# FNet mixing and an ELU layer on one core: batch 0's x by plain loads, batch 1 in the small-matmul form

## The chip, the cores and the metric

The kernel runs on one core of a Trainium2 chip. The metric is the time of one execution in device microseconds (us). Three runs of the kernel before gave 1906.94 us as the median (1906.89 to 1907.48).

## What is computed

```python
# x [8, 3008, 256] float32, w_in [256, 2048] and w_out [2048, 256] float64
X = np.fft.fft(x, axis=1)
X = np.fft.fft(X, axis=2)
t = X.real.reshape(8 * 3008, 256)
h = t @ w_in
g = np.where(h > 0.0, h, np.exp(np.minimum(h, 0.0)) - 1.0)
out = (g @ w_out).astype(np.float32)
```

A Fourier transform over the sequence and over the channels, of which the real part is kept, and then a two-layer network of width 2048 on each of the 24064 rows.

## The kernel before

**Stages.** The network takes the rows in 376 steps. A step multiplies the transformed rows by w_in (results in the PSUM bank H), applies the ELU to them (tiles E, M, G on ScalarE, VectorE and GpSimd) and multiplies G by w_out into the banks pA, pB, pC, pD. The first steps do this with plain products (`w`); later ones with sums of rows and of weights (`WT`), which need fewer products. Every step needs rows that are already transformed, so the transform of a batch must be done ahead of its steps; that of batch 0 stands ahead of everything.

**The transform of one batch.** Sequence positions s, 1504-s, 1504+s and 3008-s, for s from 0 to 752, are laid over each other, and so are channels d and 256-d. Tile `xl0` holds rows s upward, `xl1` rows 3008-s downward, `xl2` rows 1504-s downward, `xl3` rows 1504+s upward; partition p holds six rows, numbers 0 to 3 of groups of four and 4 to 5 of groups of two. Sums and differences of the four tiles and of the two channel halves give four operands of 128 x 768 (in the code `EO`). Each is multiplied by a cosine or sine table (`MC`, 128 x 1887, in an even half of 756 and an odd half of 1131 columns): R for the real and I for the imaginary part, each for even and odd frequencies. Such a product is the class `Dft`: an even half of 3 matmuls and an odd half of 3. Beside these four, `x_even` and `x_odd` transform channel 128 alone (`xe`). Batches 0 and 1 take this form. Batches 2 to 7 take another, the class `Quarter`: the sequence is folded once more, and the operands are multiplied by small tables (`QM`, 94 to 96 rows, 94 or 95 columns), 4 matmuls for a half. It costs more additions on VectorE and GpSimd (`mirror_sum`, `half_sum`, `channel_fold`, and the functions called by `quarter_pairs`, `shift_pairs`, `turn_pairs`).

**How x of batch 0 comes in.** `load_x` reads the forward rows (`xl3`, `xl0`) by two DMAs each, on SyncE's queue (SP): 128 pieces of 4 KB, and of 2 KB. The mirrored rows (`xl2`, `xl1`) are read by four gathers that GpSimd issues (`indirect_dma_start`, with row numbers in the table `ix`). `fold_x` then makes the channel sums e0 to e3 and differences o0 to o3 of each tile, and adds and subtracts these (E0, EO0 and so on), 16 VectorE instructions on 768 elements, two of them cut in two.

**Batch 1.** Its x comes by the same two kinds of load (events `L`, `L0` to `L3`). `mirror_folds` gives GpSimd 30 instructions for its sums: 12 on 255 elements of a partition, 2 small ones, 8 on 384 (the tiles), 8 on 384 (the channel halves). Its four `Dft`s stand at steps 26, 34, 37 and 42.

**Weights.** w_in and w_out are float64 in memory and are converted on chip, in chunks `w0` to `w5`, `u0` to `u5`: load, then about ten instructions on 512 elements of a partition, on VectorE, ScalarE and GpSimd (in the trace the tiles raw, w, pow).

**What sets the order.** Each piece of work has a model time (`at(t, fn)`, in steps of T); sorted by it, the pieces are written out, and every engine runs its instructions in that written order. For the first seven steps the table `FRONT` names the pieces: `e3` is one of the sums above; `x-even`, `x-odd`, `R-even` and so on are the halves of the transforms; `R-sum`, `R-up`, `R-down` combine the halves on VectorE; `w0b` is a part of a chunk; `h`, `P`, `Q`, `g`, `V`, `b`, `x` are parts of a step. PE, the matmul engine, starts with 46 matmuls on zeros (`idle`), which nothing reads.

**Waits of DMAs.** The DMAs of the SP and ScalarE queues take eight semaphores in turn (DMAHW0 to DMAHW7), so a DMA waits, before it is issued, until the one that had its semaphore has landed.

Of the kernel before, what the change touches and what calls it, by code (L numbers as in the profile page):

```python
# [17 lines left out]
SEQ = 3008  # L18
# [21 lines left out]
def _dft_consts():  # L40
# [6 lines left out]
    p = np.arange(128)[:, None]  # L47
# [130 lines left out]
def kernel(  # L178
# [33 lines left out]
    def xrows(b, row, step, n, rows=6):  # L212

        return bass.AP(
            tensor=xt,
            offset=x.offset + (b * SEQ + row) * ND,
            ap=[[step * ND, n], [1, rows * ND]],
        )


# [3 lines left out]
    def row_tables():  # L224

        for c, n, base, step in (
            (0, 128, HALF - 3, -4),
            (1, 128, HALF - 513, -2),  # L230
            (2, 128, HALF - 3, -4),
            (2, 1, HALF - 4, 0),
        ):
            pin(
                nc.gpsimd.iota(
                    ix[0:n, c : c + 1],
                    pattern=[[0, 1]],
                    base=base,
                    channel_multiplier=step,
                )  # L240
            )

    def load_x(b):
# [6 lines left out]
        def back(j, few):  # L250
            cols = slice(0, 2 * ND) if few else slice(2 * ND, 6 * ND)
            c = 1 if few else 0
            pin(
                nc.gpsimd.indirect_dma_start(
                    out=L[j][:, cols],
                    out_offset=None,
                    in_=xflat,
                    in_offset=bass.IndirectOffsetOnAxis(
                        ap=ix[:, c : c + 1].bitcast(U32), axis=0
                    ),  # L260
                    element_offset=(b * SEQ + (HALF if j == 1 else 0)) * ND,
                )
            )
        def ahead(j, row):
            nc.sync.dma_start(out=L[j][:, 0 : 4 * ND], in_=xrows(b, row, 4, 128, 4))
            nc.sync.dma_start(
                out=L[j][:, 4 * ND :], in_=xrows(b, row + 512, 2, 128, 2)
            )

        loads = [lambda n=n: back(2 - n // 2, n % 2) for n in range(4)]  # L270
        return L, loads + [lambda: ahead(3, HALF), lambda: ahead(0, 0)]


# [95 lines left out]
    class Chunk:  # L369
# [7 lines left out]
        def load(self):  # L377
# [6 lines left out]
            if not wide:  # L384
                nc.sync.dma_start(out=dst, in_=self.src)
                return
# [3 lines left out]
            nc.sync.dma_start(  # L390
                out=words.rearrange("p (a b) -> p a b", a=n), in_=self.src.bitcast(I32)
# [192 lines left out]
    row_tables()  # L584
# [115 lines left out]
    def sum_weights(i):  # L700
# [5 lines left out]
        b11, b12 = w2v[:, 2 * i, 0:128], w2v[:, 2 * i, 128:256]  # L706
        b21, b22 = w2v[:, 2 * i + 1, 0:128], w2v[:, 2 * i + 1, 128:256]
        W = [t[:, i] for t in WT]
# [6 lines left out]
    def fold_x(L, engine_of, cuts_of):  # L715

        ops = {}

        def op(key, o, a, b, f):
            tt = lambda o, a, b, f: pin(  # L720
                engine_of(key).tensor_tensor(out=o, in0=a, in1=b, op=f)  # L721
            )
            cuts = cuts_of(key, o.shape[1])
            for i in range(len(cuts) - 1):
                c = slice(cuts[i], cuts[i + 1])
                ops[key, i] = lambda c=c: tt(o[:, c], a[:, c], b[:, c], f)

        E, O = [], []
        for j in range(4):
# [6 lines left out]
            if j in (1, 2):  # L736
                src = src[:, ::-1]
# [968 lines left out]
    for load in loads[:5]:  # L1706
        load()
# [490 lines left out]
```

## Time and profile before

| what | value |
| --- | --- |
| median of three runs | 1906.94 us |
| profiled execution | 1907.16 us |
| its span in the trace | 1905.4 us, so 1.76 us lie outside |
| PE busy | 1898.3 us |
| VectorE (DVE), ScalarE (ACT), GpSimd (POOL) busy | 1232.0, 1391.4, 1353.1 us |
| granted PE clock | 1.00 |

Times are in microseconds from the start of the span, unless a column says ns. A timeline row gives start, duration, engine, source line, operation, output and input tiles, shape, count, and in brackets the idle time before it with what ended it. Where rows of one engine follow each other closely, the distance between two starts is the cost, since an instruction's own duration overlaps the next. A matmul of float32 leaves two records, so "x6" is three matmuls. A window row gives start and end, length, busy time of PE, PEld (the weight loads), DVE, ACT and POOL with their counts, the granted clock, the mean busy share of the 16 DMA engines and GB/s.

### The profile page before, as it was taken

To read this page: it belongs to the slowest core of one execution; us is meant where nothing else is said; L and a number is where in the kernel's file an instruction comes from. 1 tells how busy PE (TensorE), PEld (TensorE's weight loads), DVE (VectorE), ACT (ScalarE), POOL (GpSimd) and SP (SyncE) were. 2 spreads that over 40 slices of the span, in tenths; PEclk is the share of its full clock that TensorE was granted. 3 is DMA by queue.
4 is the path that set the end of the run, shared out by engine and by line. 5 is a ranking of instruction groups with operands and counts; after the bars stand their busy time and mean duration, and the time that the engine had idled before them with its cause. 6 is when DMAs were issued, how large, how long until landed. Compare 5 with 4: busy or idle time off the path is not lost.

```text
span 1905.4 us, 28620 instructions
## 1 busy us (share of the span) xinstructions
PE 1898.3 (100%) x8972; PEld 1656.8 (87%) x8972; DVE 1232.0 (65%) x2174; ACT 1391.4 (73%) x2803; POOL 1353.1 (71%) x1846
## 2 busy tenths in 40 slices
PE   9999999999999999999999999999999999999999
PEld 6888888888888888888888888888888888888887
DVE  8755555667666676667766677666776667655445
ACT  5767667777777777777777777777777777777775
POOL 4888658786687766777667777687766777556664
PEclk9999999999999999999999999999999999999999
DMA  8145211211011110211102111022110210100101
GB/s 340 45 33 43 55 24 45 53 24 36 12 44 41 32 33 12 47 40 30 31 19 50 35 27 31 13 56 44 24 24 16 55 21 15 17 12 15 20 11 24
DMA packets 278901, 73.66 MB, mean 39 GB/s; under 512 B 254382, under 2 KB 268972, under 8 KB 278750
## 3 DMA queue, kind: packets, MB, share of 16 engines
q1 hardware_dynamic: 270110, 61.40, 15.9%
q0 software_dynamic: 6464, 10.18, 1.7%
q8 instruction: 71, 1.16, 0.3%
q14 instruction: 80, 0.66, 0.1%
q10 hardware_dynamic: 2176, 0.26, 0.1%
HBM read 46.92 MB, written 24.80 MB: 38 GB/s over the span
## 4 chain that ended last, share of the span: by engine, by line
PE 96%; DVE 2%; ACT 1%; issue 0%; DMA 0%; POOL 0%; ACTq 0%; POOLq 0%; DVEq 0%
PE H L621 37%; PE pB L621 17%; PE pD L621 17%; PE pC L621 17%; PE pA L621 9%; DMA xl<-in_x_dram,ix 0%; DVE e L721 0%; ACT G L633 0%; DVE o L721 0%; POOL w L630 0%; DVE G L1431 0%; DVE E L1401 0%; ACT M L633 0%; ACT E L633 0%; DVE pow L462 0%
## 5 line engine op out<-in xcount | busy, mean ns | idle before, releaser
L630 POOL TENSOR_TENSOR G<-G 128x256 f32<-128x256 f32 x1437 | 1047.4, 737 | 498.0 <-DVE G L1431 358.5
L1431 DVE SCALAR_TENSOR_TENSOR G<-G,H 128x512 f32<-128x512 f32 x376 | 258.2, 687 | 554.5 <-ACT G L633 554.5
L633 ACT ACTIVATE G<-H 128x512 f32<-128x512 f32 x376 | 224.5, 597 | 259.0 <-DVE G L1415 255.4
L621 PE MATMUL H<-Rr,Wsc 128*128 128x256 f32 x1504 | 388.7, 381 | 1.0 <-ACT Wsc L633 0.5
L621 PE MATMUL H<-Ir,Wsc 128*128 128x256 f32 x1504 | 386.7, 380 | 0.7 <-DVE E L1401 0.7
L633 ACT ACTIVATE H<-Rb,wex 128x256 f32<-128x256 f32 x720 | 341.2, 474 | 40.0 <-DVE G L1431 21.5
L621 PE MATMUL pC<-G,WT 128*128 128x256 f32 x1440 | 369.8, 379 | 0.0
L633 ACT ACTIVATE E<-H 128x512 f32<-128x512 f32 x360 | 214.5, 596 | 182.0 <-PE H L621 181.7
L621 PEld LDWEIGHTS H<-Ir,Wsc 128*128 128x128 f32 x1504 | 285.6, 190 | 40.6 <-DVE E L1401 1.5
L621 PEld LDWEIGHTS H<-Rr,Wsc 128*128 128x128 f32 x1504 | 281.7, 190 | 43.1 <-issue 2.3
L621 PEld LDWEIGHTS pC<-G,WT 128*128 128x128 f32 x1440 | 274.2, 190 | 36.6
L1415 DVE SCALAR_TENSOR_TENSOR G<-E,H 128x512 f32<-128x512 f32 x376 | 255.0, 678 | 8.4 <-PE H L621 4.3
L1431 DVE SCALAR_TENSOR_TENSOR G<-M,G 128x512 f32<-128x512 f32 x376 | 256.7, 683 | 0.7 <-ACT M L633 0.7
L633 ACT ACTIVATE G<-G 128x512 f32<-128x512 f32 x376 | 235.0, 625 | 0.0
L621 PE MATMUL pA<-G,w 128*128 128x256 f32 x784 | 229.6, 380 | 0.1
L621 PE MATMUL pB<-G,w 128*128 128x256 f32 x784 | 229.5, 379 | 0.0
L621 PE MATMUL pD<-G,w 128*128 128x256 f32 x784 | 229.4, 379 | 0.0
L633 ACT ACTIVATE M<-G 128x512 f32<-128x512 f32 x376 | 224.4, 597 | 2.8 <-DVE G L1415 2.8
L633 ACT ACTIVATE M<-M 128x512 f32<-128x512 f32 x376 | 222.7, 592 | 0.1
L621 PE MATMUL pB<-G,WT 128*128 128x256 f32 x720 | 214.7, 380 | 0.0
L621 PE MATMUL pD<-G,WT 128*128 128x256 f32 x720 | 214.4, 379 | 0.0
L621 PEld LDWEIGHTS pA<-G,w 128*128 128x128 f32 x784 | 149.2, 190 | 20.6 <-DVE G L1431 0.5
(175 smaller groups left out, 1794.3 us busy)
## 6 DMA issues: line engine op xcount, KB each, us to landing
out_dram<-ot SPq DMA_DIRECT2D x496, 32.0 KB
xq<-in_x_dram SPq DMA_DIRECT2D x48, 94.0 KB
out_dram<-ot SPq DMA_DIRECT2D x256, 2.0 KB
Rb<-r SPq DMA_DIRECT2D x10, 376.0 KB
raw<-in_moe_w_in_dram SPq DMA_DIRECT2D x7, 512.0 KB
MC<-dft_mats SPq DMA_DIRECT2D x3, 943.5 KB
xq<-in_x_dram SPq DMA_DIRECT2D x12, 192.0 KB
xq<-in_x_dram SPq DMA_DIRECT2D x36, 64.0 KB
```

The lines of the kernel that those rows point to most:

```text
L621: nc.tensor.matmul(out_, lhsT=lhsT, rhs=rhs, start=start, stop=stop, skip_group_check=True)
L630: pin(nc.gpsimd.tensor_tensor(out=o, in0=a, in1=b, op=op))
L633: pin(nc.scalar.activation(out=o, in_=i, func=func, **kw))
L1415: nc.vector.scalar_tensor_tensor(out=two(S.G[:, 0:512])[:, :, ::-1], in0=two(S.E), scalar=2.0, in1=two(S.H), op0=ALU.mult, op1=ALU.subtract,)
L1431: nc.vector.scalar_tensor_tensor(out=o, in0=e, scalar=-1.0, in1=h, op0=ALU.add, op1=ALU.max)
```

## The change

**Batch 0's x.** There is no gather. Even and odd rows are loaded apart, even ones first. A forward tile comes by four SP DMAs for each parity, of 64 partitions. A mirrored tile comes by three DMAs for each parity on ScalarE's queue, of 128 partitions with 1 KB each, twelve in all. Such a source is written as two runs of 64 rows that go downward, so partition p holds what partition (p + 64) mod 128 held, and the tables `MC` are permuted alike. The cosine tables' halves are loaded apart too.

On SyncE's queue the program began so before (DMA out<-in and elements of the out tile; "waits" names a semaphore; `raw` and `w_68` are weight chunks, `CC` the channel table):

```order
L265 DMA xl_150<-in_x_dram 128x1024
L266 DMA xl_150<-in_x_dram 128x512
L390 DMA raw<-in_moe_w_in_dram 128x2x512
L265 DMA xl_147<-in_x_dram 128x1024
L266 DMA xl_147<-in_x_dram 128x512
L1710 DMA CC<-chan_mats 128x384
L554 DMA MC_73<-dft_mats 128x756
L554 DMA MC_73<-dft_mats 128x1131
L390 DMA raw<-in_moe_w_in_dram 128x2x512 [waits DMAHW0_49]
```

The two forward tiles and the first weight chunk come first there. Now SyncE's queue begins so (`xl_130` is tile 3, `xl_127` tile 0):

```order
L230 DMA xl_130<-in_x_dram 64x2x256 x2
L230 DMA xl_130<-in_x_dram 64x256 x2
L1646 DMA MC_73<-dft_mats 128x756
L230 DMA xl_127<-in_x_dram 64x2x256 [waits DMAHW2_49]
L230 DMA xl_127<-in_x_dram 64x2x256 [waits DMAHW4_49]
L230 DMA xl_127<-in_x_dram 64x256 [waits DMAHW7_49]
L230 DMA xl_127<-in_x_dram 64x256 [waits DMAHW1_49]
L1660 DMA CC<-chan_mats 128x384 [waits DMAHW3_49]
L373 DMA raw<-in_moe_w_in_dram 128x2x512 [waits DMAHW5_49]
```

Tile 0's loads now wait for loads issued earlier on either queue. ScalarE's instructions, of which only the first two stood at its start before (`xl_129` is tile 2, `xl_128` tile 1):

```order
L617 ACT_TABLE_LOAD
L617 ACTIVATE warm<-warm 128x1 [waits DVE_49]
L230 DMA xl_129<-in_x_dram 128x1x256 x3
L230 DMA xl_128<-in_x_dram 128x1x256 [waits DMAHW0_49]
L230 DMA xl_128<-in_x_dram 128x1x256 [waits DMAHW1_49]
L230 DMA xl_128<-in_x_dram 128x1x256 [waits DMAHW3_49]
L230 DMA xl_128<-in_x_dram 128x1x256 [waits DMAHW5_49]
L230 DMA xl_128<-in_x_dram 128x1x256 [waits DMAHW6_49]
L230 DMA xl_128<-in_x_dram 128x1x256 [waits DMAHW0_49]
L230 DMA xl_129<-in_x_dram 128x1x256 [waits DMAHW2_49]
L230 DMA xl_129<-in_x_dram 128x1x256 [waits DMAHW4_49]
L230 DMA xl_129<-in_x_dram 128x1x256 [waits DMAHW6_49]
```

The mirrored rows moved from GpSimd's gathers to ScalarE's queue, the first weight chunk behind the even rows, and loads of the two queues now wait for each other through the shared semaphores.

**The order of sums.** For each parity the mirrored rows are added to the forward rows first (a3, a0: 765 elements and 3), then the two tiles are added (Z0) and subtracted (Z1: 768 each), and the channel halves are folded from these (E0, O0, E1, O1: 384 each). VectorE's first rows on x before (`xl_150` is tile 3, `xl_149` tile 2, `xl_147` tile 0; e_ and o_ channel sums and differences, w_157 and pow_178 parts of chunk w0):

```order
L721 TENSOR_TENSOR e_174<-xl_150 128x768
L721 TENSOR_TENSOR o_175<-xl_150 128x768
L408 TENSOR_SCALAR pow_178<-raw 128x512
L420 TENSOR_SCALAR w_157<-raw 128x2x256
L450 SCALAR_TENSOR_TENSOR w_157<-raw,w_157 128x2x256
L462 SCALAR_TENSOR_TENSOR pow_178<-raw,pow_178 128x512
L476 SCALAR_TENSOR_TENSOR w_157<-w_157,pow_178 128x2x256
L721 TENSOR_TENSOR e_168<-xl_147 128x512
L721 TENSOR_TENSOR e_172<-xl_149 128x256
```

There the two sums of tile 3 and the chunk's conversion stand ahead of the first mirrored row (`xl_149`). VectorE's first rows now (numbers of tiles as on the queues above, `eo` an operand, w_144 and pow_211 parts of chunk w0; the rows on 3 elements leave out the last size):

```order
L611 TENSOR_TENSOR xl_130<-xl_130,xl_129 128x3x255
L611 TENSOR_TENSOR xl_130<-xl_130,xl_129 128x3
L611 TENSOR_TENSOR xl_127<-xl_127,xl_128 128x3x255
L611 TENSOR_TENSOR xl_127<-xl_127,xl_128 128x3
L611 TENSOR_TENSOR xl_128<-xl_127,xl_130 128x3x256
L611 TENSOR_TENSOR eo<-xl_128 128x3x128 x2
L405 TENSOR_SCALAR w_144<-raw 128x2x256
L393 TENSOR_SCALAR pow_211<-raw 128x512
L435 SCALAR_TENSOR_TENSOR w_144<-raw,w_144 128x2x256
L611 TENSOR_TENSOR xl_130<-xl_130,xl_129 128x3x255
L611 TENSOR_TENSOR xl_130<-xl_130,xl_129 128x3
```

The first instruction now needs both `xl3` and `xl2`, and the chunk's conversion moved behind the even rows' sums.

**PE's start.** Behind the zeros stood before (numbers of tiles: `w_157` chunk w0, `xe` channel 128, MC_73 and MC_74 the tables of even frequencies):

```order
L621 MATMUL H<-w_157,CC 128x256 x4
L621 MATMUL pC<-MC_73,xe_224 128x189 x2
L621 MATMUL pC<-MC_73,xe_224 128x378
L621 MATMUL pD<-MC_73,xe_224 128x377 x3
L621 MATMUL H<-pick,Wsc 128x1 x2
L621 MATMUL pB<-MC_73,e_170 128x377 x3
L621 MATMUL pA<-MC_73,e_170 128x189 x2
```

The weights' product stood first. Now, behind 30 instead of 46 matmuls on zeros:

```order
L605 MATMUL pC<-MC_73,xe_174 128x189 x2
L605 MATMUL pC<-MC_73,xe_174 128x378
L605 MATMUL pA<-MC_73,eo 128x189 x2
L605 MATMUL pA<-MC_73,eo 128x378
L605 MATMUL M<-MC_74,eo 128x189 x2
L605 MATMUL M<-MC_74,eo 128x378
L605 MATMUL H<-w_144,CC 128x256 x4
L605 MATMUL pD<-MC_73,xe_174 128x377 x3
L605 MATMUL pB<-MC_73,eo 128x377 x3
L605 MATMUL pC<-MC_74,eo 128x377 x3
```

The even halves of x, R and I moved ahead of the weights' product; the odd halves, which need odd rows, stand behind it.

**Batch 1** takes the class `Quarter`: `mirror_folds` and its 30 instructions go, and 16 `mirror_sum`, 8 `half_sum`, 16 `channel_fold` and 20 calls of the pair functions come, at times of the table `FIRST`; the four transforms stand at steps 23, 34, 38 and 44 (`QUARTERS`). Its loads change accordingly. `half_sum` is now one instruction in place of two (for all batches), and `sum_weights` is called four times on two chunks in place of eight times on one.

```diff
-    p = np.arange(128)[:, None]
+    p = (np.arange(128)[:, None] + 64) % 128
...
+            if j in (1, 2):
+                for m in (par, 2 + par):
+                    load(t[:, m], r0 - m - 256, [[256 * ND, 2], [-4 * ND, 64]])
+                m = 4 + par
+                load(t[:, m], r0 - 508 - m - 128, [[128 * ND, 2], [-2 * ND, 64]])
+                return
+            for a in range(2):
+                h = slice(64 * a, 64 * a + 64)
+                load(
+                    t[h, par:4:2], r0 + par + 256 * (1 - a), [[4 * ND, 64], [2 * ND, 2]]
+                )
...
-        for m in (2 * h, 2 * h + 1):
-            vtt(o[:, 3 - m], a[:, m], b[:, m], ALU.subtract if kodd else ALU.add)
+        m = slice(2 * h, 2 * h + 2)
+        tt(o[:, 2 - 2 * h : 4 - 2 * h][:, ::-1], a[:, m], b[:, m], ALU.subtract if kodd else ALU.add)
...
-    for _ in range(46):
+    for _ in range(30):
         mm(idle, zero, zero[:, 0:1].to_broadcast([128, 512]), True)
...
+    FIRST_LOADS = 'x20 x30 M000 x00 C w0 x10 x31 x11 M100 x01 M001 x21 M101 w1 p'
...
+    REST_LOADS = 'w2 u0 u2 M01 u1 w4 w3 M11 u5 w5'
...
-        (-20.84, "e3 o3"),
-        (-19.11, "w0a w0b w0p w0R c3"),
+        (-20.84, "xl1 a3e x1 a0e Z0e E0e c0e O0e"),
+        (-18.994, "m0e w0b x-even R-even w0a w0R I-even w0p"),
+        (-16.994, "x-copy a3o w0s w0M f0 a0o Z0o E0o"),
...
-    for step, ri, kodd in ((26, 0, 0), (34, 1, 0), (37, 0, 1), (42, 1, 1)):
-        at_dft(step, 2, 1, ri, kodd, lambda k=2 * ri + kodd: state["EO"][k])
...
+    QUARTERS = ((23, 1, 0, 0, 29), (34, 0, 0, 0, 38), (38, 0, 1, 43, 48), (44, 1, 1, 45, 53))
...
+    for step, ri, kodd, finish, join in QUARTERS:
+        at_quarter(step, 1, ri, kodd, finish, join)
```

In `FIRST_LOADS` a name such as `x20` is tile 2's even rows, `x21` its odd rows, `M001` the odd half of table (0, 0), `w0` a chunk, `C` the channel table.

More of the change, by code (lines that the diff above doesn't have):

```diff
@@ L210, with load_x @@
     xt = x.tensor
[L212 to L218, printed above, removed]
     xflat = x.rearrange("b s d -> (b s) d")
     ix = cpool.tile([128, 6], I32, tag="ix")
[L224 to L243, printed above, removed]
+    def load_x():
         L = [
@@ L375, in __init__, with load @@
             self.shared, self.pairs = shared, pairs
-        def load(self):
+        def load(self, keep=lambda i: i):
             dst = self.dst()
@@ L1889 @@
         at(t, lambda c=c: spread_last_row(c))
-    for i in range(8):
-        at((12.9 + 0.5 * i) * T + 3.6, lambda i=i: sum_weights(i))
+    for n, t in enumerate((13.208, 16.4467, 17.2731, 15.0726)):
+        at(t * T, lambda i=2 * n: sum_weights(i))
     total = n_tiles * 8
```

353 lines of the change are left out of this document (146 added, 207 removed), and 49 rows, old and new, of the table FRONT.

## The prediction

> **What bounds the kernel now.** I read the busy times first, then PE's waits, then the timelines of PE and VectorE over the first 45 us, then DMA windows. From the page:
>
> ```profile
> span 1905.4 us, 28620 instructions
> PE 1898.3 (100%) x8972; PEld 1656.8 (87%) x8972; DVE 1232.0 (65%) x2174; ACT 1391.4 (73%) x2803; POOL 1353.1 (71%) x1846
> ```
>
> PE is busy in all but 7 us of the span. So PE time taken out shortens the program, PE time added lengthens it, and time on other engines counts only where PE waits. PE's waits, largest first:
>
> ```profile
> PE H L621 <- ACT Wsc L633: 1.1, 2, 0.6
> PE M L621 <- DVE zero L581: 1.1, 1, 1.1
> ```
>
> But busy PE is not all useful PE. The start of its timeline, with one later piece:
>
> ```profile
> 1.14 13.12 PE L621 MATMUL M<-zero 128*128 128x512 bf16 x46 [1.14 <-DVE zero L581]
> 14.10 1.89 PE L621 MATMUL H<-w,CC 128*128 128x256 f32 x8
> 15.84 1.54 PE L621 MATMUL pC<-MC,xe 128*128 128x189 f32 x6
> 17.22 2.06 PE L621 MATMUL pD<-MC,xe 128*128 128x377 f32 x6
> 19.12 0.50 PE L621 MATMUL H<-pick,Wsc 128*128 128x1 f32 x4
> ...
> 36.14 1.89 PE L621 MATMUL pA<-G,w 128*128 128x256 f32 x8
> ```
>
> Until 14.10 PE multiplies zeros; x-even starts at 15.84, x-odd at 17.22, and the first product of a step (pA<-G) at 36.14. From there PE runs steps almost without a gap, so a shift of 36.14 goes through to the end. What sets it is VectorE, as its timeline shows:
>
> ```profile
> 5.19 0.96 DVE L721 TENSOR_TENSOR e<-xl 128x768 f32<-128x768 f32 x1 [1.86 <-DMA xl<-in_x_dram]
> 6.07 0.95 DVE L721 TENSOR_TENSOR o<-xl 128x768 f32<-128x768 f32 x1
> 6.94 0.42 DVE L408 TENSOR_SCALAR pow<-raw 128x512 int32<-128x512 int32 x1
> 7.27 0.42 DVE L420 TENSOR_SCALAR w<-raw 128x512 int32<-128x512 int32 x1
> 7.73 0.69 DVE L450 SCALAR_TENSOR_TENSOR w<-raw,w 128x512 f32<-128x512 uint32 x1
> 8.34 0.68 DVE L462 SCALAR_TENSOR_TENSOR pow<-raw,pow 128x512 int32<-128x512 int32 x1
> ...
> 10.85 0.42 DVE L721 TENSOR_TENSOR e<-xl 128x256 f32<-128x256 f32 x1 [0.30 <-DMA xl<-in_x_dram,ix]
> ...
> 25.03 0.54 DVE L627 TENSOR_TENSOR Rb<-bs,pD 128x375 f32<-128x375 f32 x1
> 25.48 0.54 DVE L627 TENSOR_TENSOR Rr<-bs,pB 128x377 f32<-128x377 f32 x1
> ...
> 27.98 0.87 DVE L1401 SCALAR_TENSOR_TENSOR E<-Rb,wex,H 128x256 f32<-128x256 f32 x2
> ...
> 34.34 0.68 DVE L1431 SCALAR_TENSOR_TENSOR G<-M,G 128x512 f32<-128x512 f32 x1
> ```
>
> VectorE works from 5.19 to the end of the first G, 35.02, with idle times of a few tenths: 0.30 for the first gather. Costs between starts: 0.87 us for 768 elements, 0.33 for TENSOR_SCALAR on 512, 0.61 for SCALAR_TENSOR_TENSOR on 512, 0.45 for 377.
>
> **The new loads.** The change takes the gathers away and puts twelve DMAs of 128 x 1 KB = 131 KB on ScalarE's queue, with a source of two runs that go downward. Before, only line 336's loads (94 rows of 1 KB, two runs of 47 downward) are alike; line 319's go forward. Windows on two times of line 336, one of line 319 (96 rows), and the start:
>
> ```profile
> 297.25:298.00 0.75, 0.75 (x5) 0.65 (x5) 0.75 (x2) 0.72 (x3) 0.64 (x1) 1.00 0.13 48
> 299.00:300.50 1.50, 1.50 (x8) 1.33 (x7) 1.12 (x3) 1.18 (x4) 1.42 (x3) 1.00 0.14 48
> 182.50:183.50 1.00, 1.00 (x6) 0.90 (x5) 0.92 (x3) 0.70 (x3) 0.98 (x2) 1.00 0.94 298
> 12.00:20.00 8.00, 7.78 (x36) 5.16 (x35) 7.93 (x16) 2.50 (x8) 0.00 (x0) 1.00 1.05 415
> ```
>
> Line 336's loads keep 0.13 of 16 engines busy, which is two, at 48 GB/s; line 319's keep 0.94 busy at 298 GB/s. The new loads lie between: their source is like the slow ones, their 128 destination rows like the fast ones. So one costs 131 KB / 48 GB/s = 2.73 us or 131 / 298 = 0.44 us. Whether 94 rows or two runs made line 336 slow, no row says, since there both go together. I take 2.73, because only those rows have the same source. The other value is rival A.
>
> The Trainium skill (DMA: Bandwidth & Descriptors, section "Why a DMA increments its semaphore by 16 and not by 1") says that a DMA takes the largest number of engines up to 16 that divides the slowest dimension, other than 1, of both sides. The source's two runs would make that two, the sum below; were the destination alone to count, it would be 16, rival A. The trace agrees at line 336 (0.13), but no run here shows 128 rows against two runs.
>
> **The front, step by step, at 2.73 us a load.** ScalarE's queue can begin behind its table load:
>
> ```profile
> 0.74 1.28 ACT L633 ACT_TABLE_LOAD   x1 [0.74 <-PEq L2182]
> 2.04 0.20 ACT L633 ACTIVATE warm<-warm 128x1 f32<-128x1 f32 x1
> ```
>
> So bytes flow from about 3.3 (an estimate: 2.24 and a second for issue and landing). Twelve loads on two engines: 32.8 us. These engines also carry their sixteenth of SyncE's part ahead of the last of them, 3.07 MB in all (the forward rows, half tables, CC, w0): 192 KB an engine at 415 / 16 = 25.9 GB/s is 7.4 us. Last odd row of `xl2`: 3.3 + 32.8 + 7.4 = 43.5. SyncE's forward rows are no help: each DMA waits for one issued eight earlier on either queue, so the last forward odd rows are issued behind the last but one of ScalarE's, and land near 45.
>
> Then a0 (0.95), Z0 (0.87) and the copy of channel 128: x-odd starts near 47.3 instead of 17.22. Even rows land earlier (six loads and half the rest, about 22.6), x-even runs near 25 instead of 15.84, and PE, with zeros until 10.6 only, stands idle around it. Behind x-odd come the odd halves of R and I, three times 1.9 us (17.22 to 19.12). R-up needs R's: 47.3 + 3.8 = 51.1, or up to 53 if PE comes slow out of its idle time. That it can be slow, the weight loads of the first zeros show:
>
> ```profile
> 6.66 0.15 PEld L621 LDWEIGHTS <-zero 128*128 128x128 bf16 x1 [0.28 <-issue]
> 7.09 6.67 PEld L621 LDWEIGHTS <-zero 128*128 128x128 bf16 x31 [0.28 <-issue]
> ```
>
> One matmul took 0.43 us until 7.09 and 6.67 / 31 = 0.22 after it. I take 1 us for it, with 0 and 2 as ends.
>
> The Trainium skill (TensorE: Matmul & The Clock Gate, Part 1) says that PE idle for a window of about 3.4 us falls back to half its clock. By it the whole 2 us would be paid here; the trace agrees in the first 14 zeros, and no row of it shows a return to the slow rate.
>
> Behind R-up, to the end of the first G, the new order has on VectorE 9 pieces of 375 to 384 elements at 0.45 (two halves of a sum counted as one), 5 TENSOR_SCALAR at 0.33, 6 SCALAR_TENSOR_TENSOR at 0.61 (of G and of weights), one 768 at 0.87, four E pieces at 0.4: 4.1 + 1.7 + 3.7 + 0.9 + 1.6 = 12.0. So G ends near 52 + 12 = 64, and the first pA starts with it: 64 - 36.1 = +28.
>
> Covers in this stretch. The remaining weights and tables (w1, w2, u0, the table M01) stand behind these loads on SyncE; they start near 45 and move at 415 GB/s: 2.6 MB by their shapes, 6.3 us, so until 52, when VectorE is at R-up. M01 is first used after it, w1 shortly before: cover nearly gone, up to +3. GpSimd loses four gathers; VectorE's 0.30 us wait was for one of them. The removed 16 zeros and the shorter sums (16 x 768 elements become 4 x 768 + 4 x 768 + 8 x 384, 4.3 us less at 0.87 for 768) lie in time when everything waits for rows, and bring nothing here.
>
> **Batch 1.** From PE's timeline: an even and an odd half of `Dft` with what followed each, and a half of `Quarter`:
>
> ```profile
> 173.00 1.44 PE L621 MATMUL H<-MC,eo 128*128 128x189 f32 x6
> 174.28 1.03 PE L621 MATMUL H<-Rr,Wsc 128*128 128x256 f32 x4
> ...
> 184.63 2.07 PE L621 MATMUL H<-MC,eo 128*128 128x377 f32 x6
> 186.54 1.03 PE L621 MATMUL H<-Rr,Wsc 128*128 128x256 f32 x4
> ...
> 442.14 0.58 PE L621 MATMUL H<-QM,e 94*128 94x95 f32 x4
> 442.56 0.61 PE L621 MATMUL H<-QM,o 94*128 94x95 f32 x4
> 443.01 1.06 PE L621 MATMUL H<-Rr,Wsc 128*128 128x256 f32 x4
> ```
>
> Four pairs of 1.28 + 1.91 go, 12.8 us; eight halves of 0.87 come, 7.0. These lie on PE, where nothing covers them: -5.8. The additional sums go to VectorE and GpSimd, in these windows; the page's row of GpSimd's sums stands with them:
>
> ```profile
> L630 POOL TENSOR_TENSOR G<-G 128x256 f32<-128x256 f32 x1437 | 1047.4, 737 | 498.0 <-DVE G L1431 358.5
> ...
> 80.00:90.00 10.00, 10.00 (x50) 7.41 (x49) 7.02 (x13) 7.43 (x14) 9.77 (x11) 1.00 0.01 0
> 100.00:110.00 10.00, 9.30 (x43) 7.91 (x42) 8.92 (x14) 5.43 (x11) 9.64 (x12) 1.00 0.30 93
> ```
>
> GpSimd is nearly full there (9.77 of 10), so its new sums must replace the 30 old ones, which go; VectorE has 1 to 3 us in 10 free. I cost the swap at 0; if GpSimd falls behind, PE waits for a sum of 0.74 us (737 ns) at one or another of batch 1's eight halves, so at most some +4. The joined `half_sum` and `sum_weights` lie on the same engines, same cover, 0.
>
> **Sum.** Against the profiled execution of 1907.16 us (0.22 above the median, 1.76 of it outside the span): +28 - 5.8 = +22, so 1929. Ends: without SyncE's share on the two engines -7.4, 1922; with late weights, a cold PE and GpSimd's waits +8, 1937.
>
> **Rivals.**
> A, faster: the new loads run at 0.44 us. Even rows (of four tiles, 1.57 MB, with a table's half of 0.39 MB) at 415 GB/s: 4.7 us from the first bytes near 3, plus landing, about 8.5. x-even then starts near 11, where the 30 zeros end (14 at 0.43 and 16 at 0.22 from 1.14: 10.6). VectorE's work from a3 on is 13.3 us with R-up (7 of 768 and four small ones 6.4; 9 of about 380, 4.1; 3 TENSOR_SCALAR, 1.0; 3 SCALAR_TENSOR_TENSOR, 1.8) and 12 as above: 8.5 + 25.3 = 33.8 instead of 35.0, -1.2 (ends 0 and -3.5, the zeros removed); -5.8 for batch 1. That is 1900, from 1896 to 1904. For it: 128 rows; at the start of before, loads of 128 rows filled all engines (share 1.05). Against: two runs.
> B, no change: loads as in A, but waits eat the 8 us. It needs GpSimd late in most of batch 1's four transforms, 2 us in each (three sums); its windows above are full, but 30 sums leave it. 1907, 1904 to 1910.
> C, slower by another way: loads as in A, but the shared semaphores decide. 32 loads of both queues stand up to the last odd row, eight can be under way, so it lands after four rounds from issue to landing. One round, from the trace of before, where e3 (5.19) waited for this load:
>
> ```profile
> 1.21 0.42 SPq L266 DMA_DIRECT2D xl<-in_x_dram  x1
> ```
>
> That is 4.0 us; four rounds from 0.75 end at 16.8, and a0 of the odd rows, behind 7.1 us of VectorE's work in A, wants them at 8.5 + 7.1 = 15.6: +1 of A's -7. From 5.8 us a round it costs the whole gain; at 7 us, when all engines are busy, the rows come at 28.8: +13 - 7 = +6, 1913.
>
> **Chances.** Forecast 0.62; A 0.32; B 0.03; C 0.03. What differs from no change by less than 0.2%, 3.8 us, a measurement of this kernel can hardly tell. Faster 0.32 (A), same 0.04 (B, a part of C), slower 0.64. The forecast's own range is 1922 to 1937. Since A has more than 2 in 10, the whole range must take in most of it: 1898 to 1936.
>
> **What would show it.** In the changed kernel's windows from 4 to 40 us: DMA share well below 1 and mean rate near 100 GB/s (the forecast), or about 1 and 400 (A). x-even at 25 or at 11, x-odd at 47 or near 17, the first pA<-G at 64 or 34. PE's busy time falls by 3.5 (zeros) and 5.8 in every case but for a slow restart. Between 110 and 260 us, PE's waits on GpSimd's sums would show B. The forecast is wrong if two runs of source do not hold a load to two engines; it is off in size if the two engines are quicker than 48 GB/s, or other queues slow them.

## The result and the profile after

The changed kernel takes 1958.42 us (median of 4 runs, 1954.21 to 1963.23) against 1906.91 us (1906.82 to 1907.48): a ratio of 1.0268, 95% interval 1.0254 to 1.0282. It is 51.5 us slower, where 22 were forecast. Two of the four runs took 1954 us and two 1963; what sets these apart stays open. The run profiled here took 1954.21 us with a span of 1952.4, 47.0 more than before. From its page:

```profile
span 1952.4 us, 28718 instructions
PE 1895.6 (97%) x8972; PEld 1653.0 (85%) x8972; DVE 1235.5 (63%) x2187; ACT 1393.9 (71%) x2813; POOL 1365.7 (70%) x1836
```

PE is busy 2.7 us less than before and stands still for 56.8 us instead of 7.1. Its waits by releaser, largest first (total, times, longest):

```profile
PE pC L605 <- ACT xe L617: 28.2, 1, 28.2
PE H L605 <- DVE E L1336: 14.8, 4, 9.0
```

The first lies in the front. The second was not in the prediction at all. PE's timeline puts both in their places:

```profile
1.14 8.01 PE L605 MATMUL M<-zero 128*128 128x512 bf16 x30 [1.14 <-DVE zero L566]
37.39 2.89 PE L605 MATMUL pC<-MC,xe 128*128 128x189 f32 x6 [28.25 <-ACT xe L617]
49.40 2.14 PE L605 MATMUL pD<-MC,xe 128*128 128x377 f32 x6 [1.01 <-DMA MC<-dft_mats]
67.48 1.96 PE L605 MATMUL pA<-G,w 128*128 128x256 f32 x8
...
84.66 1.13 PE L605 MATMUL H<-Ir,Wsc 128*128 128x256 f32 x4 [2.44 <-DVE E L1336]
85.62 3.49 PE L605 MATMUL pB<-G,w 128*128 128x256 f32 x8
...
150.24 2.08 PE L605 MATMUL H<-Ir,Wsc 128*128 128x256 f32 x4 [8.99 <-DVE E L1336]
```

The first product of a step starts at 67.48 instead of 36.14: the front costs 31.3 us. The windows at the start show the two engines of the forecast (clock, DMA share and GB/s are the last three columns):

```profile
12.00:20.00 8.00, 0.00 (x0) 0.00 (x0) 1.03 (x2) 0.00 (x0) 0.00 (x0) 0.63 0.16 55
20.00:30.00 10.00, 0.00 (x0) 0.00 (x0) 0.00 (x0) 0.00 (x0) 0.00 (x0) 0.50 0.39 128
```

For 18 us almost nothing computes, and the DMA engines are busy to 0.16 and 0.39. VectorE's timeline has the sums of these rows: a0 of the even rows, which is released by ScalarE, and a3 of the odd rows, which waits for `xl2`:

```profile
34.34 2.02 DVE L611 TENSOR_TENSOR xl<-xl,xl 128x765 f32<-128x765 f32 x3 [18.53 <-ACT xl L617]
43.98 1.03 DVE L611 TENSOR_TENSOR xl<-xl,xl 128x765 f32<-128x765 f32 x2 [5.29 <-DMA xl<-in_x_dram]
```

What a0 waits for on ScalarE is the copy of one row (`x1` in the table `FRONT`). It stands in ScalarE's order behind the issue of its loads, most of which wait for an earlier load to land. ScalarE's queue and ScalarE:

```profile
2.25 31.60 ACTq L230 DMA_DIRECT2D xl<-in_x_dram  x11
33.89 0.41 ACT L617 ACTIVATE xl<-xl 1x256 f32<-1x256 f32 x1 [31.65 <-DMA xl<-in_x_dram]
```

Where the remaining 16 us lie is seen when one instruction, VectorE's G<-G,H, is followed from step to step. Its start in us, from the timelines of six kernels (h1, e1, g3 and k3 are experiments below):

| step | before | after | e1 | h1 | g3 | k3 |
| --- | --- | --- | --- | --- | --- | --- |
| 1 | 32.62 | 65.51 | 41.43 | 32.99 | 32.51 | 32.76 |
| 4 | 50.22 | 81.31 | 57.23 | 55.09 | 50.11 | 50.36 |
| 13 | 106.74 | 157.50 | 132.84 | 126.37 | 112.01 | 111.43 |
| 21 | 147.58 | 198.96 | 174.28 | 173.23 | 158.91 | 152.27 |
| 376 | 1893.80 | 1940.63 | 1916.93 | 1914.92 | 1900.60 | 1894.00 |

After minus before is 32.9 at step 1, 31.1 at step 4, 51.4 at step 21 and 46.8 at the end. So there is a second loss of 20.3 us between steps 4 and 21, while batch 1's rows are loaded and summed (18.5 when counted from step 1; the pieces of the first steps stand in another order now), and then a gain of 4.6. SyncE's queue shows what stands ahead of the wait at 150.24. `wx` takes the last row of a scaled weight chunk to memory, `wex` spreads it over 128 partitions; VectorE's E needs it:

```profile
130.51 13.13 SPq L318 DMA_DIRECT2D xq<-in_x_dram  x3
143.74 0.42 SPq L657 DMA_DIRECT2D wx<-Wsc  x1
144.21 0.61 SPq L318 DMA_DIRECT2D xq<-in_x_dram  x1
147.00 0.39 SPq L660 DMA_DIRECT2D wex<-wx  x1
```

SyncE stands for 13.13 us at loads of batch 1's rows (`xq`). The chain of work that ended last runs through the same place; its rows name what those loads had waited for, a gather of the far rows (`in_x_dram,ix`) of 12.27 us:

```profile
130.75 12.27 DMA xq<-in_x_dram,ix
143.74 3.24 DMA wx<-Wsc
147.00 2.21 DMA wex<-wx
```

VectorE's rows show that PE's 8.99 us have two parts: VectorE waits for GpSimd's part of a weight chunk's conversion first, and E, which stands behind that, for `wex`:

```profile
141.38 0.43 DVE L393 TENSOR_SCALAR pow<-raw 128x512 int32<-128x512 int32 x1 [2.95 <-POOL w L614]
149.31 0.87 DVE L1336 SCALAR_TENSOR_TENSOR E<-Rb,wex,H 128x256 f32<-128x256 f32 x2 [6.64 <-DMA wex<-wx]
```

A further wait of PE for E, 2.56 us at 128.20, has no DMA in front of it. VectorE is simply full there, with sums of batch 1 (`xq`) among its rows (third busy time, 10.00 of 10):

```profile
120.00:130.00 10.00, 7.44 (x36) 4.82 (x36) 10.00 (x12) 4.78 (x9) 5.96 (x6) 1.00 0.00 1
```

### The profile page after: what moved, and what is told of

The parts are those of the page before. It is cut to its first block, busy times and chain, and to the rows that moved or that the text cites. A ratio compares the mean times of both kernels' runs of the same rounds, so it can differ in the third digit from the quotient of the medians.

```text
span 1952.4 us, 28718 instructions
## 1 busy us (share of the span) xinstructions
PE 1895.6 (97%) x8972; PEld 1653.0 (85%) x8972; DVE 1235.5 (63%) x2187; ACT 1393.9 (71%) x2813; POOL 1365.7 (70%) x1836
## 4 chain that ended last, share of the span: by engine, by line
PE 91%; DMA 3%; ACTq 1%; ACT 1%; DVE 1%; POOL 1%; issue 1%; SPq 0%; POOLq 0%; DVEq 0%
PE H L605 35%; PE pB L605 16%; PE pD L605 16%; PE pC L605 16%; PE pA L605 8%; ACTq L230 1%; DMA xq<-in_x_dram,ix 1%; DMA Wsc<-in_moe_w_out_dram 1%; DMA xl<-in_x_dram 1%; DMA wex<-wx 1%; POOL WT L614 0%; ACT G L617 0%; DVE G L1366 0%; POOL G L614 0%; POOL xq L614 0%
## 5 line engine op out<-in xcount | busy, mean ns | idle before, releaser
L614 POOL TENSOR_TENSOR G<-G 128x256 f32<-128x256 f32 x1437 | 1060.5, 746 | 482.7 <-DVE G L1366 348.5
L605 PEld LDWEIGHTS pB<-G,w 128*128 128x128 f32 x784 | 150.7, 192 | 21.0
```

The source lines that it names most:

```text
L605: nc.tensor.matmul(out_, lhsT=lhsT, rhs=rhs, start=start, stop=stop, skip_group_check=True)
L614: pin(nc.gpsimd.tensor_tensor(out=o, in0=a, in1=b, op=op))
```

## The experiments

The kernel before, run beside them, took 1906.98 to 1907.66 us. A time without an interval is one run.

### The front: e1, e2, e3, e5

Theory: the source's number of runs sets the number of engines that a load uses. Rivals: the downward direction of the rows is slow, or the waits on shared semaphores are. These kernels change only how a mirrored load is split, so partitions hold other rows than the tables expect. e1, sixteen runs of 8 rows:

```diff
-                    load(t[:, m], r0 - m - 256, [[256 * ND, 2], [-4 * ND, 64]])
+                    load(t[:, m], r0 - m - 480, [[32 * ND, 16], [-4 * ND, 8]])
...
-                load(t[:, m], r0 - 508 - m - 128, [[128 * ND, 2], [-2 * ND, 64]])
+                load(t[:, m], r0 - 508 - m - 240, [[16 * ND, 16], [-2 * ND, 8]])
```

> The changed kernel, with each of the twelve mirrored loads written as 16 runs of 8 downward rows in place of 2 runs of 64 (same rows, same bytes, another order over the partitions, so the sums pair other rows). Theory 'runs' (a load gets as many DMA engines as its source has runs, here 16): the first pA<-G falls from 67.5 to 34 to 37 us. Theory 'direction' (downward rows are slow whatever their runs): it stays near 67. On the second loss, 18 us between the fourth and the twelfth step: if it is made by the late front, the time is near 1900 us; if batch 1's new loads and sums make it by themselves, near 1918 to 1922.

Measured: 1928.76 us, ratio 1.0109 (1.0092 to 1.0126). PE's timeline:

```profile
15.85 2.89 PE L605 MATMUL pC<-MC,xe 128*128 128x189 f32 x6 [5.39 <-ACT xe L617]
43.41 1.96 PE L605 MATMUL pA<-G,w 128*128 128x256 f32 x8
```

x-even comes 21.5 us earlier and the first product 24.1 us earlier, by a change of nothing but the runs. e2, two runs that go upward (`[4 * ND, 64]` instead of `[-4 * ND, 64]`, likewise for `2 * ND`):

> The changed kernel, with each mirrored load as two runs of 64 rows that go upward, with a gap between the runs (other rows of x, same bytes). Theory 'runs': nothing changes, first pA<-G near 67 us, time 1950 to 1963 us. Theory 'direction': first pA near 35, time 1900 to 1922 us.

Measured: 1952.92 us in one run. PE:

```profile
37.14 2.89 PE L605 MATMUL pC<-MC,xe 128*128 128x189 f32 x6 [26.64 <-ACT xe L617]
67.58 1.97 PE L605 MATMUL pA<-G,w 128*128 128x256 f32 x8
```

As in the changed kernel, within 0.3 us: the direction has no part in it. e3, four runs (`[[128 * ND, 4], [-4 * ND, 32]]` and `[[64 * ND, 4], [-2 * ND, 32]]`):

> The changed kernel, with each mirrored load as 4 runs of 32 downward rows (rows in another order over the partitions). Theory 'runs': four engines, so the twelve loads take 16.4 us in place of 32.8; the first pA<-G falls from 67.5 to about 51 and the time by 16 us or somewhat more, to about 1936. Theory 'direction': no change, about 1955 to 1963 us.

Measured: 1936.69 us, and on PE:

```profile
22.05 2.89 PE L605 MATMUL pC<-MC,xe 128*128 128x189 f32 x6 [11.48 <-ACT xe L617]
50.85 1.96 PE L605 MATMUL pA<-G,w 128*128 128x256 f32 x8
```

Two, four and sixteen runs give 67.5, 50.9 and 43.4. The Trainium skill (DMA: Bandwidth & Descriptors, section "Why a DMA increments its semaphore by 16 and not by 1") has the rule that the largest number up to 16 that divides the slowest dimension of both sides is the number of engines; these three kernels agree with it.

Still, with sixteen runs the front is 7.3 us behind that of before. Is that the rounds through the shared semaphores? e5 is e1 with fewer loads: the forward tile comes by two DMAs of 128 partitions for each parity, not four of 64.

```diff
-            for a in range(2):
-                h = slice(64 * a, 64 * a + 64)
-                load(
-                    t[h, par:4:2], r0 + par + 256 * (1 - a), [[4 * ND, 64], [2 * ND, 2]]
-                )
+            load(t[:, par:4:2], r0 + par, [[4 * ND, 128], [2 * ND, 2]])
...
-            for a in range(2):
-                h = slice(64 * a, 64 * a + 64)
-                load(t[h, m], r0 + 508 + m + 128 * (1 - a), [[2 * ND, 64]])
+            load(t[:, m], r0 + 508 + m, [[2 * ND, 128]])
```

> The changed kernel with mirrored loads of 16 runs (1928.8 us), with each forward tile's rows of a parity in two DMAs of 128 partitions in place of four of 64 (8 DMAs fewer ahead of the last odd row; other rows beside each other, so the output is another). If rounds of eight DMAs through the shared semaphores hold up the even rows (there until 12.8 us): x-even 2 to 4 us earlier than 15.85, first pA<-G near 40 in place of 43.4, 1925 to 1927. If bytes alone hold them up: unchanged, 1928 to 1931.

Measured: 1927.54 us in one run.

```profile
17.37 2.89 PE L599 MATMUL pC<-MC,xe 128*128 128x189 f32 x6 [7.85 <-ACT xe L611]
42.72 1.97 PE L599 MATMUL pA<-G,w 128*128 128x256 f32 x8
```

x-even is later, not earlier, and the first product 0.7 us earlier. So eight loads fewer bring back a tenth of the 7.3 us; the rounds of the mirrored loads themselves are as they were. The windows of e1 show something else:

```profile
4.00:8.00 4.00, 4.00 (x14) 1.59 (x13) 1.03 (x2) 0.00 (x0) 0.00 (x0) 1.00 0.97 281
8.00:12.00 4.00, 2.46 (x12) 0.88 (x10) 0.00 (x0) 0.00 (x0) 0.00 (x0) 1.00 0.79 233
```

From 4 to 8 us all engines are busy (0.97) and move 281 GB/s. Before, with rows of 4 and 2 KB, they moved 375 in the same window, at a share of 1.03:

```profile
4.00:8.00 4.00, 4.00 (x12) 1.49 (x11) 2.77 (x5) 0.61 (x1) 2.37 (x3) 1.00 1.03 375
```

Rows loaded by parity come in pieces of 1 KB. That the size of the pieces makes the difference was not tried.

### Batch 1 by itself: h1

Theory: the second loss comes with the new form of batch 1, wherever the front ends. Rival: it follows from the late front. h1 is the kernel before, with batch 1's new loads, sums and transforms at the changed kernel's times and with `half_sum` as one instruction. The front and the eight calls of `sum_weights` are those of before.

```diff
+    names["L"] = lambda: [load_next(0), load_next(3)]
+    names["L0"] = lambda: [quarter_table(), load_next(2)]
...
-    for step, ri, kodd in ((26, 0, 0), (34, 1, 0), (37, 0, 1), (42, 1, 1)):
-        at_dft(step, 2, 1, ri, kodd, lambda k=2 * ri + kodd: state["EO"][k])
...
+    FAR_LOADS, MIRROR, HALVES, FOLDS, PAIRS = FIRST
...
+    for step, ri, kodd, finish, join in QUARTERS:
+        at_quarter(step, 1, ri, kodd, finish, join)
```

> The kernel before, with batch 1 alone in the small-matmul form (its loads, sums and transforms at the times of the changed kernel, half_sum as one instruction); the front with gathers stays. If the second loss of 18 us is a consequence of the late front: only PE's 5.8 us go, 1901 us. If batch 1's new loads and sums make it by themselves (weight rows wx and wex waiting on SyncE's queue behind batch 1's loads): +18 - 5.8, about 1919 us.

Measured: 1929.49 us, ratio 1.0115 (1.0098 to 1.0132). That is 10 us more than the expected 1919. In the table above 20.8 us are lost between steps 4 and 21, where the changed kernel loses 20.3 and e1 19.7. So such a loss comes without the late front. It isn't the same loss in every part: h1 has lost another 4.5 us between steps 1 and 4, at the wait at 54.63 below, so from step 1 to 21 it loses 25.3 and the changed kernel 18.5. PE's timeline and SyncE's queue:

```profile
36.51 1.89 PE L621 MATMUL pA<-G,w 128*128 128x256 f32 x8
54.63 2.08 PE L621 MATMUL H<-Ir,Wsc 128*128 128x256 f32 x4 [3.74 <-DVE E L1401]
...
119.42 2.07 PE L621 MATMUL H<-Ir,Wsc 128*128 128x256 f32 x4 [8.62 <-DVE E L1401]
```

```profile
100.11 12.74 SPq L336 DMA_DIRECT2D xq<-in_x_dram  x3
112.96 0.41 SPq L673 DMA_DIRECT2D wx<-Wsc  x1
116.36 0.39 SPq L676 DMA_DIRECT2D wex<-wx  x1
```

The gather, on GpSimd, was issued at 100.34; behind it stood three loads of rows, behind these `wx`, then `wex`, E and PE. One window of h1 shows the third party, GpSimd, which never rests (fifth busy time, 9.84 of 10), though PE waits:

```profile
110.00:120.00 10.00, 1.38 (x5) 0.88 (x4) 2.79 (x6) 4.03 (x8) 9.84 (x12) 0.79 0.31 95
```

Two theories from here, the weight row behind the loads, and GpSimd too full. The rest of the runs start from h1.

### Moving the queue or the sums: f1, f2, f3

f1 puts the weight row on ScalarE's queue:

```diff
-        pin(nc.sync.dma_start(out=wx_dr[:, c], in_=Ws[127:128, c]))
+        pin(nc.scalar.dma_start(out=wx_dr[:, c], in_=Ws[127:128, c]))
...
-                nc.sync.dma_start(
+                nc.scalar.dma_start(
...
+        at(t + 2.0, lambda c=c: spread_columns(c))
```

> The kernel with batch 1 alone changed (1929.5 us), with the two small transfers that spread the last weight row of a chunk (wx, wex) moved from SyncE's to ScalarE's queue, wex 2 us of model time behind wx. Theory 'queue' (these transfers stand on SyncE behind batch 1's loads, and VectorE's E, then PE, wait for them: 3.7 and 8.6 us of PE's waits and a slow clock behind each): both waits go, 1929.5 - 12 = 1917. Theory 'sums' (GpSimd and VectorE have too much work in steps 7 to 12): 1925 to 1930.

Measured: 1927.69 us (1922.23 to 1929.37), ratio 1.011 (1.0093 to 1.0127). PE:

```profile
62.97 1.13 PE L621 MATMUL H<-Rr,Wsc 128*128 128x256 f32 x4 [3.55 <-ACT Wsc L633]
...
113.12 2.08 PE L621 MATMUL H<-Ir,Wsc 128*128 128x256 f32 x4 [3.52 <-DVE E L1404]
```

This is the run of 1922.23 us, 5.5 below the median. The wait of 8.62 is 3.52 in it, but a new one of 3.55 stands before it, for ScalarE's scaled weights: a DMA that waits holds up ScalarE's own work as well (2.59 us at 59.61, behind `wex`, which waits for `wx`). f2 keeps SyncE and moves batch 1's sums and loads 2.5 steps back:

```diff
+    later = lambda t: t + 2.5 if t < 30 else t
...
-    QUARTERS = ((23, 1, 0, 0, 29), (34, 0, 0, 0, 38), (38, 0, 1, 43, 48), (44, 1, 1, 45, 53))
+    QUARTERS = ((26, 1, 0, 0, 29), (34, 0, 0, 0, 38), (38, 0, 1, 43, 48), (44, 1, 1, 45, 53))
```

> The same kernel (1929.5 us), with batch 1's sums, far loads and pairs 2.5 steps later (those planned before step 30) and its first transform at step 26 in place of 23; wx and wex stay on SyncE. Theory 'sums': the loss at the ninth step (4.8 us) and part of that at the twelfth go, 1917 to 1922. Theory 'queue': the 3.7 us wait stays, for the near loads do not move; the 8.6 us wait goes only as far as the far loads now stand behind the weight rows: 1920 to 1925.

Measured: 1936.16 us, 1.015 (1.0133 to 1.0167), worse. PE, and SyncE's queue:

```profile
141.71 2.07 PE L621 MATMUL H<-Ir,Wsc 128*128 128x256 f32 x4 [18.04 <-DVE E L1401]
```

```profile
120.56 13.32 SPq L1214 DMA_DIRECT2D x<-in_x_dram  x2
133.92 1.29 SPq L673 DMA_DIRECT2D wx<-Wsc  x1
```

The same hold-up at another place: SyncE stands 13.32 us at other loads of x, and `wx` behind them. f3 does both edits.

> Both edits together. If queue and sums are the whole second loss: 1907.2 - 5.8 = 1901, up to 1906. If something else of batch 1's form costs time: above 1910.

Measured: 1939.35 us, 1.017 (1.0153 to 1.0187). With the weight row out of that queue PE's largest wait is 11.98 us for a sum of GpSimd's. Neither edit, nor both, gives the time back; moving work only chooses which engine is late.

### Taking work away: f4, g1, g2, g3

These leave out parts of batch 1's transform. f4 replaces its far gathers by plain forward loads:

> The kernel with batch 1 alone changed (1929.5 us), with batch 1's two far gathers replaced by plain forward loads of the same size (other rows of x, so batch 1's output is another). If SyncE stands still because its odd-row loads wait for a gather that takes 12.3 us to land: the 8.6 us wait at the twelfth step falls by most of it, 1921 to 1923. If the gather only looks slow because GpSimd issues it late: 1927 to 1930.

```diff
+            if far and b == 1:
+                for p, k in ((0, 80), (80, 14)):
+                    nc.sync.dma_start(
...
+                return
```

Measured: 1926.82 us. The wait of 8.62 is 2.84 now, so the gather was behind most of it, but other waits grow and only 2.7 us come back. g1 leaves out the 16 `mirror_sum`s:

```diff
-    for n, t in enumerate(MIRROR):
...
-        at(t * T, lambda n=n, far=far: mirror_sum((0, 3)[n // 4], far, (0, 2, 1, 3)[n % 4]))
```

> The kernel with batch 1 alone changed (1929.5 us), with batch 1's 16 mirror sums on GpSimd left out (12 us of its work in steps 7 to 18; batch 1's output is another). Theory 'sums' (GpSimd and VectorE overfull): the losses at the ninth step (4.8) and at the seventeenth to nineteenth (5.6) go, and a part of that at the twelfth: 1916 to 1920. Theory 'queue': the waits for the weight row stay, 1925 to 1929.

Measured: 1920.81 us, 8.7 less than h1, although the wait on the weight row stays:

```profile
116.37 2.07 PE L621 MATMUL H<-Ir,Wsc 128*128 128x256 f32 x4 [8.97 <-DVE E L1401]
```

g2 keeps the sums and loads all of batch 1's tiles by plain forward loads, of 4 KB pieces (`ap=[[8 * ND, k], [1, 4 * ND]]`; `load_odd` does nothing for it):

> The same kernel (1929.5 us), with each tile of batch 1 loaded by plain forward loads of 4 KB pieces on SyncE (one of 96 partitions, or one of 80 and one of 14): no gather, no load from two runs, no load that waits for a gather (other rows of x, so batch 1's output is another). Theory 'queue': both waits for the weight row go (3.7 and 8.6, and the slow clock behind them, 3 us): 1913 to 1916. Theory 'sums': 1925 to 1929.

Measured: 1917.73 us, 11.8 less than h1; its largest wait for E is 5.57. g3 does both:

> Both together. If loads and sums are the whole second loss: 1907.2 - 5.8 = 1901, up to 1905. If a cause is missing: above 1908.

Measured: 1913.98 us, 15.5 less than h1. By themselves 8.7 and 11.8 would make 20.5, so the two causes share some of their time. The longest wait for E that is left in g3 is 4.80 us on PE.

### All of it: k1, k3, and a version to keep: k4, k5

k1 is h1 without the weight row of chunks 2 to 7 (a zero in its place):

```diff
+    nc.vector.memset(wex, 0.0)
...
-        at(t, lambda c=c: spread_last_row(c))
```

> The kernel with batch 1 alone changed (1929.5 us), with the small transfers of the last weight row (wx, wex) left out for chunks 2 to 7 (these columns of wex stay 0, so the output is another). If the weight row behind batch 1's loads on SyncE is the main cause: both E waits (3.7 and 8.6) and the slow clock behind them go, 1913 to 1916. If E waits for GpSimd's work as much as for wex: 1920 to 1926.

Measured: 1919.96 us, 9.5 less than h1. Both waits for `wex` are gone. PE's and VectorE's timelines have what came in their place:

```profile
142.97 1.19 PE L622 MATMUL pA<-G,w 128*128 128x256 f32 x2 [3.52 <-DVE G L1432]
```

```profile
140.70 0.93 DVE L628 TENSOR_TENSOR xq<-xq,xq 94x512 f32<-94x512 f32 x1 [7.59 <-POOL xq L631]
```

VectorE waits 7.59 us, at a sum of batch 1, for a sum of GpSimd's; G of the step is behind it in VectorE's order, and PE waits for G. k3 takes everything away at once: g3, without the weight row, and with the copies of `channel_edge` moved from ScalarE to GpSimd. What it keeps of the change is the half sums, the folds, the pair functions and the new transforms, with plain loads.

```diff
-        act(o[:, :, 0, 63:64], lines(1 + kodd, far)[0:n, ::-1, 0:1])
+        pin(
+            nc.gpsimd.tensor_copy(
+                out=o[:, :, 0, 63:64], in_=lines(1 + kodd, far)[0:n, ::-1, 0:1]
+            )
+        )
```

> The kernel with plain loads and without mirror sums (1914.0 us), also without wx and wex, and with the edge copies (channel 0 of a fold) on GpSimd in place of ScalarE, so that ScalarE no longer waits there for GpSimd's folds. If these are the rest: 1901 to 1904. If GpSimd's folds themselves hold the weights' conversion and so PE: 1906 to 1911.

Measured: 1907.79 us, no different from before (1907.66 beside it) and 21.7 less than h1. Between steps 4 and 21 it still loses 4.6 us (table). Its longest wait there on PE, and VectorE's row ahead of that E:

```profile
104.45 2.07 PE L635 MATMUL H<-Ir,Wsc 128*128 128x256 f32 x4 [2.53 <-DVE E L1419]
```

```profile
102.32 0.43 DVE L421 TENSOR_SCALAR pow<-raw 128x512 int32<-128x512 int32 x1 [3.45 <-POOL w L644]
```

The weight row isn't there any more, and still E is late: VectorE waits for GpSimd's part of a weight chunk's conversion, and GpSimd has folds of batch 1 before and between its instructions on that chunk. VectorE itself is full shortly before, busy 10.00 and 9.88 of 10 from 70 to 80 and 80 to 90 us, where it had 8.79 and 7.02 in the kernel before. So what k3 keeps of the new form costs the 4.5 us that the smaller transforms give back from step 21 on; even without its gathers, two-run loads and mirror sums it gains nothing here. Which of the sums left costs how much was not separated.

Whole times hide where each of these runs loses. Here is what the start of G<-G,H loses against before, in us:

| steps | after | h1 | g1 | g2 | g3 | k1 | k3 |
| --- | --- | --- | --- | --- | --- | --- | --- |
| 1 to 16 | 17.86 | 19.25 | 16.77 | 15.18 | 11.43 | 7.52 | 4.54 |
| 16 to 21 | 0.63 | 6.03 | 0.02 | 0.00 | 0.01 | 9.74 | 0.01 |
| 21 to 376 | -4.55 | -4.53 | -4.51 | -4.52 | -4.53 | -4.56 | -4.49 |

The loss from step 16 to 21 is h1's own: VectorE waits there for a sum of GpSimd's (5.08 us at 150.17), and the changed kernel loses 0.63. Whether the joined `sum_weights`, which h1 lacks, spares it that was not tried. So of g1's 8.7 us only 2.5 lie in the steps in which the changed kernel loses its time, and of g2's 11.8 only 4.1. k1 gives 11.7 there, more than half of h1's loss, and loses 3.7 more behind it.

k4 is meant to be kept: h1, with the weight row made by a small matmul (functions that chunks 0 and 1 have already) instead of two DMAs, and the edge copies on GpSimd as in k3.

```diff
-    for c, t in ((2, 15.2435), (3, 23.1265)) + tuple((c, (2 * c - 1) * T + 0.04) for c in range(4, 8)):
-        at(t, lambda c=c: spread_last_row(c))
+        at((2 * c - 1) * T + 1.5, lambda c=c: turn_last_row(c))
+        at((2 * c - 1) * T + 2.6, lambda c=c: put_last_row(c))
```

> The kernel with batch 1 alone changed (1929.5 us), computing the reference: the weight row of chunks 2 to 7 is turned into columns by two small matmuls and a copy, as chunks 0 and 1 do, in place of wx and wex (about 0.45 us of PE for each of six chunks, +2.7), and the edge copies stand on GpSimd. If the weight row is the main cause: 1929.5 - 15 + 2.7 = 1917 or less. If GpSimd's work decides: 1922 to 1928.

Measured: 1921.84 us, 1.0079 (1.0061 to 1.0097): 7.7 less than h1 and still slower than before. As in k1, VectorE waits (7.34 us) for GpSimd's sum of `xq`, and PE 3.26 for G; both lie between steps 16 and 21, where k4 loses 8.1. k4's edit on top of the changed kernel, which hardly loses there, was not tried. k5 moves the sums as f2 did:

> The same, with batch 1's sums, far loads and pairs 2.5 steps later and its first transform at step 26. With the weight row off SyncE the 18 us wait of the earlier run with later sums has no place to arise: 1906 to 1911, which is the best that these causes allow; slower than 1915 would mean that GpSimd's sums are late in any order.

Measured: 1935.5 us, 1.0147 (1.0129 to 1.0166). PE's timeline, and GpSimd's:

```profile
161.58 1.22 PE L621 MATMUL pB<-G,WT 128*128 128x256 f32 x2 [18.22 <-POOL G L630]
```

```profile
150.30 0.72 POOL L630 TENSOR_TENSOR xq<-xq,xq 94x255 f32<-94x255 f32 x1 [13.15 <-DMA xq<-in_x_dram]
```

GpSimd itself waits 13.15 us for loaded rows, and the G sums behind it hold PE for 18.22. No version found beats the kernel before.

## Why the prediction was right in its direction and wrong in its size

**Loads on two engines: right.** The last odd rows let a3 start at 43.98 (forecast 43.5), x-odd ran at 49.40 (47.3). The Trainium skill's rule on engines, named at e3, had been open because no run showed 128 rows against two runs; e1, e2 and e3 agree with it. The direction alone would not show this: with the loads on all engines (e1) the kernel is slower than before as well.

**x-even: wrong, without effect.** 37.39, forecast 25. The forecast counted the landing of the even rows alone, 22.6; by the semaphores in the trace the last of them landed at 25.2. What held the sum a0 until 34.34 was ScalarE's copy of one row, at 33.89 behind its twelve loads. The end of the front goes by the odd rows, as forecast.

**The front: +31.3, forecast +28.** x-odd started 2.1 us later than forecast, with a wait of 1.01 for its table that the forecast did not have. R-up ran at 53.48 (52 was taken), and from there to the end of the first G VectorE took 13.85 us instead of 12.0. PE was slow out of its idle time, as x-even's 2.89 us instead of 1.54 show, but that lies ahead of the odd rows and costs nothing.

**Batch 1: the step that failed.** "I cost the swap at 0", and "at most some +4". It cost 20.3 us. The prediction set the new sums against the 30 old ones without adding up their time: to step 60's G<-G,H VectorE is busy 220.54 us before and 250.21 in h1 (60 instructions more), GpSimd 250.68 and 261.87. And it gave no word to batch 1's loads, nor to what is queued behind them: `wx` and `wex` stand behind loads on SyncE that wait for a gather. h1 shows a loss of this kind without the new front. Up to step 16, of its 19.3 us, k1 gives 11.7 for the weight row, g2 4.1 for the loads, g1 2.5 for the mirror sums, and k3 14.7 for all together. These overlap, so the weight row is the largest part and not the only one; none of these edits was made to the changed kernel itself. What was said of GpSimd, "if GpSimd falls behind, PE waits for a sum", named one path only. The others are VectorE waiting for GpSimd's sum with G behind it (k1), and VectorE waiting for GpSimd's part of a weight chunk's conversion, with E behind it (the changed kernel at 141.38, and k3 at 102.32).

**The smaller transforms: right in themselves.** -5.8 was forecast from eight halves; from step 21 on the changed kernel gains 4.6 (h1 4.5, k3 4.5). Added up over steps 21 to 76 by the distances between starts, the products of `Dft` took 12.70 us before and those of `Quarter` take 6.92, which is the forecast's 5.8. The missing 1.2 us lie in front of other matmuls; what holds these up stays open.

**PE's busy time: -2.7, forecast -9.3.** The zeros fell by more than forecast, 13.12 to 8.01. Against that stands work at a slow clock behind the new waits: x-even's 2.89 us instead of 1.54, 3.49 us at 85.62 for eight matmuls that take 1.9, 2.08 at 150.24 for four that take 1.03. These are not all of the difference; the rest was not added up.

**Rival A was wrong too.** It priced batch 0's even rows at 415 GB/s, the rate from 12 to 20 us, when weights and tables came in; while x came in, before moved 375 and e1 moves 281. With sixteen runs the front still cost 7.3 us, so rival A's gain was not there with these loads. Rival C had the right sign for that case, but eight loads fewer (e5) brought back only 0.7 us. By C's own numbers the gain is used up at 5.5 us, not 5.8. Rival B named GpSimd, which is one of the causes, but at the four transforms; the loss lies ahead of them, at two and a half times B's 8 us.

**The sum.** 31.3 and 20.3 less 4.6 make 47.0, the difference of the two spans. The reason for gathers of 12.3 us stays open.

## What to carry to other kernels

When a change adds transfers to a queue, list what already stands behind them in it and who waits for that, however small: here a row of 1 KB behind three loads held PE for 9 us. Before pricing a strided load by the best rate in the trace, look at its outermost count on the source side, and at the size of its pieces. When an engine reads 9.8 of 10 busy, exchanging 30 sums for others is no swap at zero: add up the time on every engine that takes them, and see who waits for each.

## What was not expected of the hardware

- With 128 rows of destination, the number of the source's runs set the rate: 2, 4 and 16 runs gave a first product at 67.5, 50.9 and 43.4 us.
- Loads mostly in pieces of 1 KB kept 0.97 of the engines busy at 281 GB/s (e1, 4 to 8 us), where pieces of 4 and 2 KB had 375 at 1.03.
- A small copy on ScalarE waited 31.65 us although the even rows had landed by 25.2 by the trace's semaphores, since it stood behind loads that ScalarE had yet to issue.
- A short wait can slow PE. After 2.53 us (k3, 104.45) four matmuls took 2.07 us, twice the 1.03 of others alike, and after 2.44 us (84.66 in the changed kernel) the eight at 85.62 took 3.49. The granted clock was 0.50 from 104.45 to 107.00 in k3 and 0.63 from 84.66 to 89.00 in the changed kernel. The same length doesn't always do it; from PE's timeline of the changed kernel, after 2.56 us:

```profile
128.20 1.13 PE L605 MATMUL H<-Ir,Wsc 128*128 128x256 f32 x4 [2.56 <-DVE E L1336]
129.17 1.89 PE L605 MATMUL pB<-G,w 128*128 128x256 f32 x8
```

The Trainium skill (TensorE: Matmul & The Clock Gate, "Part 1: The HAM clock gate (the "warmup" mystery)") puts the return to the slow clock at an idle window of about 3.4 us, and calls that window free-running. The measured 2.44 and 2.53 us are shorter than it, so here the measurement differs from what the Trainium skill states. That not every wait of this length is followed by slow work (the granted clock was 1.00 from 128 to 131 us) agrees with a window that runs by itself.
